# Halved first transposes, ScalarE key zeroing, one-step key copies and a new instruction order in a two-layer sliding-window attention and token-mixing kernel

## The chip, the cores and the metric

The kernel runs on one core of a Trainium2 chip. The metric is the device time of one execution in microseconds (us), the median of several runs. The core has five engines with a queue of instructions each: TensorE (PE in the profile, its weight loads PEld), VectorE (DVE), ScalarE (ACT), GpSimd (POOL) and SyncE (SP, which issues the DMAs here). Every queue is served in order; engines wait for each other through semaphores.

## The reference

```python
def _A_ref(x, wqkv, wo):                      # S=2048, D=512, H=32 heads of 16, window W=256
    q, k, v = split(x @ wqkv)
    scores = einsum("bhqd,bhkd->bhqk", q, k) * 16 ** -0.5
    scores = where(0 <= i - j < 256, scores, -1e9)
    return einsum("bhqk,bhkd->bhqd", softmax(scores), v) @ wo
def _B_ref(x, w1, b1, w2, b2):                # an MLP over the tokens, F=1792
    u = gelu(einsum("bsd,sf->bdf", layernorm(x), w1) + b1)
    return (einsum("bdf,fs->bds", u, w2) + b2).transpose(0, 2, 1)
for _ in range(2):
    x = x + _A_ref(layernorm(x), A_wqkv, A_wo)
    x = x + _B_ref(layernorm(x), B_w1, B_b1, B_w2, B_b2)
```

Inputs, weights and output are bfloat16; both layers use the same weights.

## The kernel before

The tokens are 16 blocks of 128 (`x_sb`, `xh_sb` after the layer norm). Four blocks make a group `m`. For each group `qkv` transposes the normalised blocks into `xhT`, multiplies them with the query, key and value weights (line 527, through `mm_group`), and copies the products out of PSUM. There are four head groups `o` of eight heads. Queries go to `qT` (lines 587 on VectorE, 589 on ScalarE). Keys go to `kbd`, where the two heads of each 32 rows stand in separate columns with zeros between: for the first group straight from PSUM, each head's columns multiplied with a 0/1 column `par` (line 598 on VectorE, two instructions, or 597 on ScalarE); for later groups by way of a staging tile `stg` (lines 609, 611) and then by POOL or VectorE (624) or by eight DMAs of SP (619). The DMAs write only what is not zero, so their tiles are zeroed once (`zero_keys`, line 506). Values go to `vst` (644, 646) and from there by DMA to `vb`.

Layer 0 takes its first group in two halves. Blocks 0 to 3 are transposed by TensorE through PSUM (line 563) and copied to `xhT` (572 on VectorE, 574 on ScalarE); all others are transposed by DMA (556). Before the first data come, TensorE multiplies a tile of ones (`f_warm`, line 397; `keep_warm`, line 404).

Attention goes over chunks of queries: 4, 4, 8, 8, 4 and 4 blocks of 64 in layer 0 and four times 8 in layer 1. For each chunk and head group TensorE makes scores (706), ScalarE the exponentials in passes of up to 1,024 columns (721, 152 in each layer), POOL multiplies the masked parts with 0/1 integers `ldm` (742), TensorE multiplies with the values (759), and VectorE and POOL transpose and divide (797, 801, 803, 808). The output product with `wo_sb` is added to `x_sb` (830), followed by the second layer norm (476, 479, 493, 500). The token MLP's first product is made in parts: `u_part` (527, summed up at 894, 896 and 898) runs between the scores of later chunks; `u_last` (909) takes the rest after the last attention chunk, followed by the GELU on ScalarE (924). `y_block` makes the second product and adds it to `x_sb` (950). Layer 0's output blocks `y` are made just ahead of layer 1's attention and between its scores.

The order of all this is not that of the program text. The text only lists operations with what they read and write, and for many of them which engines could take them (`alts`). `ORDER` is a packed list that gives, operation by operation, which comes next and on which engine; `replay` follows it, gives out tiles and PSUM banks from pools in that order, and `emit` writes one queue for each engine with the waits that the reads and writes need. The costs and priorities in the text have been used to make the list, and are not read when the kernel is built.

## Time and profile before

| | us |
|---|---|
| median of 3 runs | 434.19 |
| lowest, highest | 433.92, 434.27 |
| the profiled execution | 434.22 |
| its span in the trace | 432.5 |
| busy: PE, ACT, DVE, POOL | 413.7, 324.3, 302.8, 240.2 |

Times in the profile count from the start of the span. A row of the timeline gives start, length, engine, line, operation and tiles, how many instructions were merged, and in brackets how long the engine had been idle and what ended the idle time. In a group of instructions the number behind the bar is the busy time in us, and then the mean length of one in ns. In a table of stages, each engine's busy time is followed by its number of instructions.

### The profile page before, as it was taken

To read this page: it belongs to the slowest core of one execution; us is meant where nothing else is said; L and a number is where in the kernel's file an instruction comes from. 1 tells how busy PE (TensorE), PEld (TensorE's weight loads), DVE (VectorE), ACT (ScalarE), POOL (GpSimd) and SP (SyncE) were. 2 spreads that over 40 slices of the span, in tenths; PEclk is the share of its full clock that TensorE was granted. 3 is DMA by queue.
4 is the path that set the end of the run, shared out by engine and by line. 5 is a ranking of instruction groups with operands and counts; after the bars stand their busy time and mean duration, and the time that the engine had idled before them with its cause. 6 is when DMAs were issued, how large, how long until landed. Compare 5 with 4: busy or idle time off the path is not lost.

```text
span 432.5 us, 14247 instructions
## 1 busy us (share of the span) xinstructions
PE 413.7 (96%) x6120; PEld 188.5 (44%) x6192; DVE 302.8 (70%) x566; ACT 324.3 (75%) x375; POOL 240.2 (56%) x359
## 2 busy tenths in 40 slices
PE   8888999999999999999999999999999999999997
PEld 7444344443444444443444444443443444444454
DVE  7999988998789878647555877888876377421224
ACT  4999999999998965608989999999999960430000
POOL 5688969687797651012677589778784741000000
DMA  8744613540222446435353340320221455682353
GB/s 245 208 62 90 158 37 65 111 101 15 77 52 52 135 141 180 119 90 153 72 148 66 86 124 2 79 46 7 55 64 38 110 147 156 186 230 77 116 165 109
DMA packets 95023, 45.12 MB, mean 104 GB/s; under 512 B 27888, under 2 KB 94960, under 8 KB 94960
## 3 DMA queue, kind: packets, MB, share of 16 engines
q1 hardware_dynamic: 94960, 44.20, 39.9%
q8 instruction: 49, 0.80, 0.8%
q14 instruction: 14, 0.11, 0.1%
HBM read 33.56 MB, written 2.10 MB: 82 GB/s over the span
## 4 chain that ended last, share of the span: by engine, by line
PE 83%; ACT 8%; DVE 4%; issue 2%; POOL 1%; DMA 1%; SPq 0%
PE PS L527 58%; PE PS L706 10%; PE PS L759 8%; PE PS L909 8%; ACT pt L721 7%; POOL pt L742 1%; DVE xh_sb L500 1%; DMA x_sb<-in_A_x_dram 1%; DVE rl L797 1%; ACT kbd L597 0%; DVE x_sb L950 0%; DVE stats L476 0%; DVE uT L898 0%; DVE oT L808 0%; ACT vst L646 0%
## 5 line engine op out<-in xcount | busy, mean ns | idle before, releaser
L721 ACT ACTIVATE pt<-PS 128x1024 bf16<-128x1024 f32 (+1 forms) x304 | 282.8, 1031 | 9.5 <-PE PS L706 7.7
L742 POOL TENSOR_TENSOR pt<-pt,ldm 128x256 int32<-128x256 int32 (+2 forms) x266 | 176.5, 691 | 56.0 <-ACT pt L721 52.3
L527 PE MATMUL PS<-xh_sb,w1b 128*128 128x512 bf16 x273 | 68.9, 380 | 2.9 <-issue 2.3
L527 PE MATMUL PS<-uT,w2b 128*128 128x512 bf16 (+2 forms) x298 | 66.8, 359 | 1.0 <-issue 0.6
L527 PE MATMUL PS<-xhT,wqkv 128*128 128x512 bf16 (+1 forms) x272 | 64.2, 355 | 3.2 <-issue 1.7
L706 PE MATMUL PS<-qT,kbd 32*128 32x64 bf16 (+4 forms) x1552 | 60.2, 247 | 2.6 <-ACT pt L721 1.6
L950 DVE SCALAR_TENSOR_TENSOR x_sb<-PS,b2col,x_sb 128x512 bf16<-128x512 f32 x31 | 22.7, 747 | 55.7 <-PE PS L527 55.5
L493 POOL TENSOR_TENSOR rstd<-agg,mhalf 128x2 f32<-128x2 f32 (+1 forms) x34 | 23.5, 693 | 57.0 <-DVE agg L479 56.8
L706 PEld LDWEIGHTS PS<-qT,kbd 32*128 32x128 bf16 x1552 | 22.7, 92 | 61.2 <-ACT pt L721 44.8
L797 DVE STREAM_TRANSPOSE rl<-PS 128x1024 f32<-128x1024 f32 x31 | 38.5, 1242 | 14.1 <-PE PS L759 13.7
L759 PE MATMUL PS<-pt,vb 64*17 64x128 bf16 (+4 forms) x3104 | 44.0, 248 | 1.2 <-ACT pt L721 0.9
L476 DVE BATCH_NORM_STATS2 stats<-x_sb 128x6 f32<-128x512 bf16 x62 | 41.0, 676 | 1.4 <-DMA x_sb<-in_A_x_dram 1.1
L527 PEld LDWEIGHTS PS<-uT,w2b 128*128 128x128 bf16 x308 | 27.6, 98 | 31.9 <-issue 3.3
L527 PE MATMUL PS<-uT,pt 128*128 128x512 bf16 x164 | 40.1, 379 | 0.3 <-issue 0.2
L759 PEld LDWEIGHTS PS<-pt,vb 64*17 64x17 bf16 x3104 | 31.5, 84 | 17.9 <-ACT pt L721 6.2
L527 PEld LDWEIGHTS PS<-xh_sb,w1b 128*128 128x128 bf16 x292 | 24.6, 97 | 32.8 <-issue 5.4
L527 PEld LDWEIGHTS PS<-xhT,wqkv 128*128 128x128 bf16 x288 | 24.3, 97 | 28.8 <-issue 5.4
L909 PE MATMUL PS<-xh_sb,w1b 128*128 128x512 bf16 x154 | 34.7, 379 | 0.1
L527 PE MATMUL PS<-wqkv,xhT 128*128 128x512 bf16 x118 | 32.7, 381 | 1.9 <-ACT pt L721 1.1
L924 ACT ACTIVATE uT<-rl,b1col 128x512 bf16<-128x512 f32 x28 | 18.1, 711 | 21.7 <-DVE rl L920 21.5
L527 PE MATMUL PS<-wo_sb,oT 128*128 128x512 bf16 x118 | 31.5, 380 | 1.6 <-issue 0.8
L500 DVE TENSOR_SCALAR xh_sb<-x_sb,agg,rstd 128x512 bf16<-128x512 bf16 x64 | 28.7, 473 | 2.6 <-POOL rstd L493 2.5
(70 smaller groups left out, 330.5 us busy)
## 6 DMA issues: line engine op xcount, KB each, us to landing
w1b<-in_B_w_dram SPq DMA_DIRECT2D x109, 128.0 KB, 2.7
w2b<-in_B_w_dram SPq DMA_DIRECT2D x70, 128.0 KB, 2.8
pt<-in_B_w_dram SPq DMA_DIRECT2D x42, 128.0 KB, 3.0
vb<-vst SPq DMA_DIRECT2D x64, 68.0 KB, 2.1
out_dram<-x_sb SPq DMA_DIRECT2D x15, 128.0 KB, 1.9
x_sb<-in_A_x_dram SPq DMA_DIRECT2D x3, 512.0 KB, 7.5
wqkv<-in_A_wqkv_dram SPq DMA_DIRECT2D x4, 256.0 KB, 5.2
wqkv<-in_A_wqkv_dram SPq DMA_DIRECT2D x1, 512.0 KB, 6.6
```

Source lines behind the costliest of these rows:

```text
L476: op("vector:stat", lambda e: e.bn_stats(st[:, 0:6], bank(ft) if ft else x_sb[:, t, :]), reads=[ft or f"x{t}"], writes=[("st", i)], cost=d ...
L493: op("gpsimd:rstd", lambda e: e.tensor_tensor(rstd[:, t0:t1, 0], agg[:, t0:t1, 1], mhalf[:, 0:1].to_broadcast([P, t1 - t0]), op=ALU.pow), ...
L500: op("vector:xh", lambda e: e.tensor_scalar(xh_sb[:, t, :], x_sb[:, t, :], agg[:, t, 0:1], rstd[:, t, :], op0=ALU.subtract, op1=ALU.mult), ...
L527: return e.matmul(o, lhsT=w, rhs=x, start=start, stop=stop, skip_group_check=True)
L706: last = e.matmul(bank(tt[r // 2], r % 2)[:, base + c0 * 64:base + (c0 + n) * 64], lhsT=kbd[32 * r:32 * r + 32, tk[0][o].slot, jj].rearran ...
L721: op("scalar:exp", lambda e, ts=ts, tp=tp, i=i, cols=cols: e.activation(probs(tp)[:, i, 0:cols, :], pair(ts)[:, :, 0:cols].rearrange("p r ...
L742: return e.tensor_tensor(v, v, m, op=ALU.mult)
L759: last = e.matmul(bank(t, h)[32 * r:32 * r + 17, i + q0 * 64:i + (q0 + n) * 64], lhsT=vb[64 * h:64 * h + 64, tk[1].slot, jj, 4 * o + r, :] ...
L797: op("vector:od", lambda e, t=tod, tr=tr: e.transpose(rl[:, tr.slot:tr.slot + 2].rearrange("p a b -> p (a b)"), pair(t)), reads=[(tod, i) ...
L909: last = e.matmul(bank(tu, tt), lhsT=v()[:, sc - b0, k0 + tt * P:k0 + (tt + 1) * P], rhs=xh_sb[:, sc, :], start=(sc == b0), stop=(sc == NT ...
L924: op("scalar:gelu", lambda e, ft=ft, tt=tt: e.activation(uT[:, ft, :], rl[:, tmps[tt].slot], ACTF.Gelu_apprx_tanh, bias=b1col[:, ft:ft + 1 ...
L950: op("vector:resy", lambda e: e.scalar_tensor_tensor(x_sb[:, t, :], bank(ft), b2col[:, t:t + 1], x_sb[:, t, :], op0=ALU.add, op1=ALU.add), ...
```

## The change

- The transposes of blocks 0 and 1 and their copies to `xhT` are done in two halves of two 128-column pieces each, in banks of their own. The four copies are ScalarE's in the new list; before, one was ScalarE's and one VectorE's.
- The key and query products of the first half group for head group 0 are made 128 tokens at a time (16 matmuls of 128 columns for 8 of 256); the first 128 tokens' product reads block 0 alone.
- The zeroing of two thirds of `kbd` moves from POOL (two memsets after block 1's normalisation) to ScalarE (two copies of a zero, spread over 2,048 float32, right after the first table load).
- A first-group key copy on VectorE becomes one product of the PSUM tile, read twice, with `par`, instead of two instructions.
- The two sums that made `half` become four memsets of 64 rows, which need no other data. The last mask pieces and the ones of `vst` may go to the other of VectorE and POOL, and do. The warm-up has 36 matmuls instead of 40.
- `ORDER` is new, from the first instruction to the last. On SP the first key weights now go ahead of blocks 2 and 3, the value weights ahead of the second halves of the key and query weights. In all, ScalarE has 8 query copies less, 3 key stagings more and 3 value copies more (VectorE the reverse), and one copy of an MLP part less; POOL has 4 instructions of key spreading less, VectorE 6 more, and one key tile less is spread by DMA. Exponentials, masks and matmuls are the same in number, but for the halved first products and the warm-up.

```diff
--- before.py
+++ after.py
@@ -13,32 +13,33 @@
 
 
 ORDER = (
...
 )
 
 def begin_order(n):
@@ -393,7 +394,7 @@
         warm = Tile(banks)
 
         def f_warm(e):
-            for _ in range(40):
+            for _ in range(36):
                 last = e.matmul(PS[:, warm.slot, 0:P], lhsT=uT[:, 0, 0:P], rhs=uT[:, 0, 0:P], start=True, stop=True)
             return last
         def keep_warm(n, after):
@@ -443,13 +444,15 @@
 
 
         for h in range(2):
-            op("vector", lambda e, h=h: e.tensor_reduce(
+            f_par = lambda e, h=h: e.tensor_reduce(
                 par[:, h:h + 1], ident[:].rearrange("p (a b) -> p a b", b=32)[:, :, 16 * h:16 * h + 16],
-                axis=mybir.AxisListType.XY, op=ALU.add), reads=["ident"], writes=[("par", h)])
-            op("vector", lambda e, h=h: e.tensor_reduce(
-                half[:, h:h + 1], ident[:, 64 * h:64 * h + 64], axis=mybir.AxisListType.X, op=ALU.add),
-               reads=["ident"], writes=[("half", h)])
-        HALF = [("half", h) for h in range(2)]
+                axis=mybir.AxisListType.XY, op=ALU.add)
+            op("vector:par", f_par, reads=["ident"], writes=[("par", h)], cost=200)
+        for h in range(2):
+            for i in range(2):
+                f_half = lambda e, h=h, i=i: e.memset(half[64 * i:64 * i + 64, h:h + 1], float(i == h))
+                op("vector:half", f_half, writes=[("half", h, i)], cost=60)
+        HALF = [("half", h, i) for h in range(2) for i in range(2)]
         op("gpsimd", lambda e: e.memset(tri[:], 1.0), writes=["tri"], cost=200)
         op("gpsimd", lambda e: e.affine_select(tri[:], tri[:], pattern=[[-1, 192]], compare_op=ALU.is_ge, fill=0.0,
                                                base=31, channel_multiplier=1), reads=["tri"], writes=["tri"], cost=300)
@@ -459,8 +462,8 @@
                                                       op0=ALU.mult, op1=ALU.add), reads=["tri", "ld0"] + HALF,
            writes=["ld0"])
         for i, m, c in ((1, 1.0, 0.0), (2, -1.0, 1.0), (3, -1.0, 1.0)):
-            op("vector", lambda e, i=i, m=m, c=c: e.tensor_scalar(ldm[:, i, :], ldm[:, 0, :], m, c, op0=ALU.mult, op1=ALU.add),
-               reads=["ld0"], writes=[f"ld{i}"])
+            f_ld = lambda e, i=i, m=m, c=c: e.tensor_scalar(ldm[:, i, :], ldm[:, 0, :], m, c, op0=ALU.mult, op1=ALU.add)
+            op("vector:ldm", f_ld, reads=["ld0"], writes=[f"ld{i}"], cost=190, alts=[("gpsimd", f_ld, 280)])
         LD = [f"ld{i}" for i in range(4)]
 
         f_one = lambda e: e.memset(vst[:, :, :, :, 16:17], 1.0)
@@ -501,11 +504,6 @@
                                                       op0=ALU.subtract, op1=ALU.mult),
                reads=[f"x{t}", f"ag{t}", f"rs{t}"], writes=[f"xh{t}"], cost=dve_cost(512, 0.25, ptrs=2), lock=True)
 
-        def zero_keys():
-            for k in (1, 2):
-                op("gpsimd:zero", lambda e, k=k: e.memset(kbd[:, 4 * k:4 * k + 4].rearrange("p a b c d -> p (a b c d)").bitcast(dt.float32), 0.0),
-                   reads=["xh1"], writes=["kz0"], cost=1900)
-
         def filler(wide):
             return Tile(banks, 1, None if wide else "f")
 
@@ -554,24 +552,26 @@
                 t = 4 * m + i
                 if wide is None:
                     op("sync:tr", lambda e: e.dma_start_transpose(xhT[:, tx.slot, :, i * P:(i + 1) * P], xh_sb[:, t, :]),
-                       reads=[f"xh{t}"], writes=[(tx, i)], dma=True, cost=1700, issue=1600.0, prio=-1e5)
+                       reads=[f"xh{t}"], writes=[(tx, i, c) for c in range(4)], dma=True, cost=1700, issue=1600.0, prio=-1e5)
                     return
-                ft = filler(True)
-
-                def f_tr(e):
-                    for c in range(4):
-                        last = e.transpose(bank(ft).bitcast(dt.bfloat16)[:, c * P:(c + 1) * P],
-                                           xh_sb[:, t, c * P:(c + 1) * P], ident[:])
-                    return last
-                op("tensor:ftr", f_tr, reads=[f"xh{t}", "ident"], writes=[ft], cost=4 * 60, prio=fprio(),
-                   holds=[tx], cfg="f", cls="f")
-                if wide and not layer and m == 0:
-                    keep_warm((2, 8)[i], [g.ops[-1]])
-                src = lambda: bank(ft).bitcast(dt.bfloat16)[:, 0:512].rearrange("p (c n) -> p c n", c=4)
-                dst = lambda: xhT[:, tx.slot, :, i * P:(i + 1) * P]
-                op("vector:evt", lambda e: e.tensor_copy(dst(), src()), reads=[ft], writes=[(tx, i)],
-                   cost=dve_cost(512, 0.5, psum=True), prio=-2e5,
-                   alts=[("scalar", lambda e: e.copy(dst(), src()), act_cost(512))])
+                for c0, c1 in ((0, 2), (2, 4)) if wide and not layer else ((0, 4),):
+                    ft = filler(True)
+
+                    def f_tr(e, c0=c0, c1=c1, ft=ft):
+                        for c in range(c0, c1):
+                            last = e.transpose(bank(ft).bitcast(dt.bfloat16)[:, c * P:(c + 1) * P],
+                                               xh_sb[:, t, c * P:(c + 1) * P], ident[:])
+                        return last
+                    op("tensor:ftr", f_tr, reads=[f"xh{t}", "ident"], writes=[ft], cost=(c1 - c0) * 60, prio=fprio(),
+                       holds=[tx], cfg="f", cls="f")
+                    if wide and not layer and m == 0 and c1 == 4:
+                        keep_warm((2, 8)[i], [g.ops[-1]])
+                    src = lambda ft=ft, c0=c0, c1=c1: bank(ft).bitcast(dt.bfloat16)[:, c0 * P:c1 * P].rearrange("p (c n) -> p c n", n=P)
+                    dst = lambda c0=c0, c1=c1: xhT[:, tx.slot, c0:c1, i * P:(i + 1) * P]
+                    op("vector:evt", lambda e, src=src, dst=dst: e.tensor_copy(dst(), src()), reads=[ft],
+                       writes=[(tx, i, c) for c in range(c0, c1)],
+                       cost=dve_cost((c1 - c0) * P, 0.5, psum=True), prio=-2e5,
+                       alts=[("scalar", lambda e, src=src, dst=dst: e.copy(dst(), src()), act_cost((c1 - c0) * P))])
 
             def proj(o, which, a, b, wide):
 
@@ -579,10 +579,11 @@
                 ft = key[0]
                 at = lambda: bank(ft)[:, 0:n]
                 ts = Tile(p_stg) if which and m else None
-                mm_group("fk" if which else "fq", key, 4, lambda c: (
-                    at(), wqkv[:, c, which * 512 + o * P:which * 512 + (o + 1) * P], xhT[:, tx.slot, c, a:b]),
-                    [(tx, i) for i in range(a // P, b // P)] + [(f"w{which}", o)], cols=n, step=2 if n > 256 else 4,
-                    holds=([ts] if ts else []) + [tk[o]] if which else [tq[o]])
+                for a1, b1 in ((a, a + P), (a + P, b)) if wide and not layer else ((a, b),):
+                    mm_group("fk" if which else "fq", key, 4, lambda c, a1=a1, b1=b1: (
+                        bank(ft)[:, a1 - a:b1 - a], wqkv[:, c, which * 512 + o * P:which * 512 + (o + 1) * P], xhT[:, tx.slot, c, a1:b1]),
+                        [(tx, i, c) for i in range(a1 // P, b1 // P) for c in range(4)] + [(f"w{which}", o)], cols=b1 - a1, step=2 if b1 - a1 > 256 else 4,
+                        holds=([ts] if ts else []) + [tk[o]] if which else [tq[o]])
                 if which == 0:
                     op("vector:evq", lambda e: e.tensor_copy(qT[:, tq[o].slot, a:b], at()), reads=[key],
                        writes=[(tq[o], k) for k in KEYS(a, b)], cost=dve_cost(n, psum=True), prio=-2e5,
@@ -591,18 +592,22 @@
                 dst = lambda h: kbd[:, tk[o].slot, a // 64:b // 64, h, :]
                 if m == 0:
                     src = lambda: at().rearrange("p (s n) -> p s n", n=64)
-                    for hs in ([0], [1]) if wide and not layer else ([0, 1],):
-                        def f_ka(e, act=False, hs=hs):
-                            for h in hs:
-                                last = (e.activation(dst(h), src(), ACTF.Copy, scale=par[:, h:h + 1]) if act else
-                                        e.tensor_scalar(dst(h), src(), par[:, h:h + 1], 0.0, op0=ALU.mult, op1=ALU.add))
-                            return last
-                        two = [("vector", f_ka, len(hs) * dve_cost(n, psum=True, ptrs=1)),
-                               ("scalar", lambda e, f_ka=f_ka: f_ka(e, True), len(hs) * act_cost(n, 1))]
-                        if not wide or hs == [1]:
-                            two.reverse()
-                        op(two[0][0] + ":evka", two[0][1], reads=[key] + [("par", h) for h in hs],
-                           writes=[(tk[o], h, k) for h in hs for k in KEYS(a, b)], cost=two[0][2], prio=-3e5, alts=two[1:])
+                    heads = lambda x: x.rearrange("p s (h n) -> p s h n", h=1).to_broadcast([P, (b - a) // 64, 2, 64])
+
+                    def f_kv(e):
+                        return e.tensor_tensor(
+                            kbd[:, tk[o].slot, a // 64:b // 64], heads(src()),
+                            par[:].rearrange("p (s h n) -> p s h n", s=1, n=1).to_broadcast([P, (b - a) // 64, 2, 64]), op=ALU.mult)
+
+                    def f_ka(e):
+                        for h in range(2):
+                            last = e.activation(dst(h), src(), ACTF.Copy, scale=par[:, h:h + 1])
+                        return last
+                    two = [("vector", f_kv, dve_cost(2 * n, psum=True)), ("scalar", f_ka, 2 * act_cost(n, 1))]
+                    if not wide:
+                        two.reverse()
+                    op(two[0][0] + ":evka", two[0][1], reads=[key] + [("par", h) for h in range(2)],
+                       writes=[(tk[o], h, k) for h in range(2) for k in KEYS(a, b)], cost=two[0][2], prio=-3e5, alts=two[1:])
                     if wide:
                         first_k[0] = g.ops[-1]
                     return
@@ -638,7 +643,7 @@
                     sp, ft = sp0 + k, filler(m == 0)
                     mm_group("fv", ft, 4, lambda c, sp=sp, ft=ft: (
                         bank(ft), xhT[:, tx.slot, c, sp * P:(sp + 1) * P], wqkv[:, c, 1024:1536]),
-                        [(tx, sp)] + [("w2", o) for o in range(4)], holds=[tv, ts])
+                        [(tx, sp, c) for c in range(4)] + [("w2", o) for o in range(4)], holds=[tv, ts])
                     src = lambda ft=ft: bank(ft).rearrange("p (r h e) -> p h r e", h=2, e=16)
                     dst = lambda k=k: vst[:, ts.slots[k], :, :, 0:16]
                     op("vector:evv", lambda e, src=src, dst=dst: e.tensor_copy(dst(), src()), reads=[ft, "one"], writes=[(ts, k)],
@@ -658,8 +663,6 @@
                 late_stats[:] = [first_k[0]] if m == 0 and not layer and not first else []
                 before([4 * m + i for i in range(a // P, b // P)], first)
                 late_stats[:] = []
-                if first and not layer:
-                    zero_keys()
                 for i in range(a // P, b // P):
                     transpose(i, first if m == 0 and not layer else None)
                 for which in (1, 0):
@@ -955,6 +958,10 @@
         for layer in range(2):
             tqs, tks, tos, gate = {}, {}, {}, []
             op("scalar:tab", lambda e: e.preload_act_table_set("natural_log_exp_and_others"), writes=["acttab"], cost=1280)
+            for k in () if layer else (1, 2):
+                keys = lambda k=k: kbd[:, 4 * k:4 * k + 4].rearrange("p a b c d -> p (a b c d)").bitcast(dt.float32)
+                op("scalar:zero", lambda e, keys=keys: e.copy(keys(), stats[:, 0, 0, 6:7].to_broadcast([P, 2048])),
+                   reads=["eps0", "acttab"], writes=["kz0"], cost=1900, alts=[("gpsimd", lambda e, keys=keys: e.memset(keys(), 0.0), 1900)])
 
             def prepare(m):
                 def before(ts, wide):
```

53 lines of the change are left out of this document (27 added, 26 removed).

## The prediction

> **What bounds the kernel now.** I read the page first, then the busy time of each engine by stage, then ScalarE's instructions in order of time to find the edges of the stages, and last the start instruction by instruction.
>
> ```profile
> span 432.5 us, 14247 instructions
> PE 413.7 (96%) x6120; PEld 188.5 (44%) x6192; DVE 302.8 (70%) x566; ACT 324.3 (75%) x375; POOL 240.2 (56%) x359
> ACT  4999999999998965608989999999999960430000
> ...
> 12.00:20.00 8.00, 7.39 (x91) 3.97 (x89) 7.69 (x23) 7.98 (x12) 6.86 (x9) 1.00 0.75 212
> 20.00:40.00 20.00, 17.32 (x430) 8.45 (x430) 18.96 (x37) 19.57 (x23) 15.89 (x23) 1.00 0.43 72
> 60.00:80.00 20.00, 19.48 (x344) 8.32 (x347) 16.89 (x31) 19.45 (x22) 15.02 (x24) 1.00 0.38 69
> 120.00:140.00 20.00, 19.04 (x419) 8.04 (x403) 18.09 (x33) 18.38 (x21) 17.22 (x24) 1.00 0.21 50
> 140.00:160.00 20.00, 19.20 (x432) 9.22 (x437) 15.02 (x27) 18.25 (x20) 13.05 (x18) 1.00 0.43 120
> 260.00:280.00 20.00, 19.57 (x345) 8.42 (x347) 16.55 (x31) 19.59 (x23) 16.16 (x25) 1.00 0.18 40
> 380.00:400.00 20.00, 19.89 (x93) 9.00 (x94) 3.02 (x5) 2.73 (x5) 0.00 (x0) 1.00 0.53 150
> ```
>
> The columns of the stages are length, then busy time of PE, PEld, DVE, ACT, POOL. "ACT 75%" hides two kinds of stage. In both attentions ScalarE is busy 19.45 to 19.59 of 20 us, and VectorE is nearly as full in the first of them (18.96). In the MLP stages ScalarE does next to nothing and TensorE runs 19.89 of 20. TensorE's 96% is no proof that it binds everywhere: a busy matmul may be waiting in its pipe. So I treat an attention as a queue of ScalarE work and an MLP as a queue of matmuls; the edges are the first and last exponentials of each layer:
>
> ```profile
> 9.68 1.02 ACT L721 ACTIVATE pt<-PS 128x1024 bf16<-128x1024 f32 x1
> 157.63 1.94 ACT L721 ACTIVATE pt<-PS 128x1024 bf16<-128x1024 f32 x2 [0.22 <-PE PS L706]
> 198.37 1.94 ACT L721 ACTIVATE pt<-PS 128x1024 bf16<-128x1024 f32 x2
> 344.51 5.61 ACT L721 ACTIVATE pt<-PS 128x1024 bf16<-128x1024 f32 x6
> ```
>
> That cuts the span into a start (to 9.68), attention 0 (to 157.63 + 1.94 = 159.57), MLP 0 up to layer 1's first exponential (198.37), attention 1 (to 344.51 + 5.61 = 350.12) and the tail (to 432.5). The profiled execution took 434.22, 1.7 more than its span; the median of the three runs is 434.19, so a change of the span is read as a change of the time.
>
> **The start.** Ten rows carry it:
>
> ```profile
> 0.78 1.28 ACT L957 ACT_TABLE_LOAD   x1 [0.78 <-PEq L1017]
> 4.99 0.21 DVE L456 TENSOR_SCALAR ldm<-tri,half 128x64 int32<-128x64 bf16 x1
> 5.12 0.41 DVE L500 TENSOR_SCALAR xh_sb<-x_sb,agg,rstd 128x512 bf16<-128x512 bf16 x1
> 6.02 0.59 ACT L574 COPY xhT<-PS 128x512 bf16<-128x512 bf16 x1 [3.95 <-PE PS L563]
> 6.69 0.41 DVE L572 COPY xhT<-PS 128x512 bf16<-128x512 bf16 x1
> 7.80 1.21 PEld L527 LDWEIGHTS PS<-xhT,wqkv 128*128 128x128 bf16 x12 [0.33 <-DMA wqkv<-in_A_wqkv_dram]
> 7.80 0.84 ACT L597 ACTIVATE kbd<-PS,par 128x256 bf16<-128x256 f32 x2 [1.19 <-PE PS L527]
> 8.53 0.37 ACT L589 CAST qT<-PS 128x256 bf16<-128x256 f32 x1
> 9.22 0.40 PE L706 MATMUL PS<-qT,kbd 32*128 32x256 bf16 x12
> 12.48 1.29 DVE L476 BATCH_NORM_STATS2 stats<-x_sb 128x6 f32<-128x512 bf16 x2 [0.21 <-DMA x_sb<-in_A_x_dram]
> ```
>
> The second block's copy ends at 6.69 + 0.41 = 7.10, the keys follow, and then TensorE waits until 7.80 for the query weights to land. This wait is what the halves run into. In the new program the query weights are still fifth in SP's queue, behind the same bytes (blocks 0 and 1, the first key weights, blocks 2 and 3; the last two have changed places), so I leave their landing at 7.80.
>
> Step by step in the new lists: the mask instruction at 4.99 goes ahead of the statistics, so block 0 is normalised some 0.1 earlier. All four half copies are ScalarE's. Its casts of 256 columns take 0.37, and the next instruction after such a cast starts 0.27 later (row at 10.64 below). Begun at about 5.9, with the second pair when block 1's transposes come at 6.5, they end near 7.2: where VectorE ended at 7.10. The halves therefore give nothing here, and cost at most 0.1. The first key product ends at about 7.7 and its copies run 7.8 to 8.6, as now. The query product begins at 7.80 again, eight matmuls of 128 columns for four of 256, and the same streamed columns. What changes is behind it: only one key group, not two, stands before the first score, and VectorE, not ScalarE, copies the queries (8.5 to 8.9). ScalarE no longer has the second key pair either. I get scores at 9.05 for 9.22 and the first exponential at 9.5: **−0.2**.
>
> In SP's queue the second half of the query weights falls from seventh to ninth, behind the value weights and blocks 4 to 7. The same bytes ended at 12.48 for those blocks, so it lands there; its first score feeds ScalarE's fourth group, at 15.5 or later (two full passes, two half ones, two value copies, two full passes after 9.5): hidden. The output weights fall behind four transposes; the first product with them waits for the first chunk's outputs.
>
> Zeroing on ScalarE: two copies of 2,048 float32. The nearest rows are the POOL memset of the same tile and ScalarE's pass over 1,024 elements twice:
>
> ```profile
> 6.23 1.80 POOL L506 MEMSET kbd<- 128x2048 f32 x1 [0.51 <-DVE xh_sb L500]
> 13.02 1.80 POOL L506 MEMSET kbd<- 128x2048 f32 x1
> 10.64 0.37 ACT L589 CAST qT<-PS 128x256 bf16<-128x256 f32 x1
> 9.43 1.65 DVE L598 TENSOR_SCALAR kbd<-PS,par 128x256 bf16<-128x256 f32 x4
> L898 DVE TENSOR_TENSOR uT<-PS,uT 128x512 f32<-128x512 f32 x14 | 9.4, 672 | 4.0 <-PE PS L527 4.0
> L624 POOL TENSOR_SCALAR kbd<-stg,par 128x512 bf16<-128x512 bf16 x30 | 20.4, 695 | 1.4 <-DVE stg L609 1.2 <-ACT stg L611 0.2
> ```
>
> One copy is thus 1.80 to 1.94, both 3.6 to 3.9, from the table load's end at 2.06 to 5.7 or 6.0. Behind them on ScalarE stands the first half copy, at about 5.9; behind that TensorE. I take 1.85 each, an end at 5.8, and nothing lost; the worst is 0.1. Without the 3.95 idle before ScalarE's first copy it would cost all 3.7.
>
> One-step key copies: two VectorE instructions of 0.41 (1.65 for four) become one product of 512 written elements, nearest to the addition from PSUM of 512 at 0.672: 0.15 less per tile, seven tiles in layer 0, about 1 us of VectorE. The new order spends it: over both layers eight query copies leave ScalarE for VectorE, and three stagings and three value copies come back. Constants (the two sums replaced by four small memsets, the mask signs moved to POOL) lie before the first block's data or under the first exponentials: nothing.
>
> **Attention 0.** Between the first and the last exponential the old list gives ScalarE one narrow query copy, four wide ones and three value copies; the new one four key stagings, one wide query copy and three value copies.
>
> ```profile
> 107.49 0.61 ACT L589 CAST qT<-PS 128x512 bf16<-128x512 f32 x1
> 120.15 0.59 ACT L646 CAST vst<-PS 128x512 bf16<-128x512 f32 x1
> 294.64 0.62 ACT L611 CAST stg<-PS 128x512 bf16<-128x512 f32 x1
> 195.87 1.27 ACT L597 ACTIVATE kbd<-PS,par 128x512 bf16<-128x512 f32 x2 [4.16 <-PE PS L527]
> 385.54 10.74 PE PS L527 x49
> ```
>
> Eight against eight, a narrow one (0.27) replaced by a wide one (0.6): **+0.3**, as ScalarE is full.
>
> **MLP 0.** A group of two matmuls is 2 x 10.74 / 49 = 0.44. From the last score to the key group that releases the copy at 195.87 the old list has 47 output and 2 value groups, the new one 46 and 4; the rest is equal: one group more, 0.44. ScalarE now has two value copies right before the key copy, which are done about 0.1 late: **+0.5**.
>
> **Attention 1.** ScalarE's other instructions inside it are 13 before (2 value copies, a key activation, 5 query, 2 staging, 3 MLP) and 12 after (4, 1, 3, 1, 3): one less, **−0.6**. **The tail** keeps eight MLP groups behind the last score, not ten: 2 x 0.44, **−0.9**, as long as TensorE has work until the last four blocks are normalised. If that chain decides, it is 0.
>
> Sum: −0.2 + 0.3 + 0.5 − 0.6 − 0.9 = −0.9, 434.2 − 0.9 = **433.3**. Upwards the tail's term may be 0 and copies and zeroing cost 0.1 each; downwards the first score may be ready with its keys (8.6) instead of its queries (8.9), 0.3 earlier: 433.0 to 434.4.
>
> **The rivals.** *VectorE becomes the bound of the first chunks (slower).* It is 18.96 of 20 full between 20 and 40 us. Up to the 32nd exponential the new list has four query copies more and one statistic more on it, and is 1.1 us longer by the rows above (one-step copies included). If every us of lateness becomes a wait of a score, that is +1.1 there and again about 1 while later key and query copies stay late: 433.3 + 2.1 = 435.4. For it speaks the fullness; against it that by the 64th exponential the new list is 1.7 shorter again. It decides once ScalarE falls below 19 of 20 in that stage.
>
> *POOL's relief shortens the waits (faster).*
>
> ```profile
> L759 PEld LDWEIGHTS PS<-pt,vb 64*17 64x17 bf16 x3104 | 31.5, 84 | 17.9 <-ACT pt L721 6.2 <-POOL pt L742 6.1 <-issue 3.9
> 0.86 0.08 DVE L470 MEMSET stats<- 128x24 f32 x1 [0.86 <-PEq L1017]
> 0.91 0.17 DVE L407 MEMSET uT<- 128x128 bf16 x1
> 1.10:2.10 1.00, 0.96 (x10) 1.00 0.27 40
> 4.60:5.10 0.50, 0.50 (x10) 1.00 1.03 309
> ```
>
> The value products wait 6.1 us for POOL's masks. POOL loses 3.6 of zeroing and four instructions of key spreading (2.8). From 120 to 160 ScalarE idles 1.62 + 1.75; if a third of that goes, and ScalarE's list keeps its place in attention 1, some 1.1 more comes off: 432.2. Against it: early masks are not what the first scores wait for.
>
> *The array is slow at the first products.* The last two rows (length, PE busy, clock, DMA) show warm-up matmuls at about 0.1 us apiece at the start and 0.05 later, with a granted clock of 1.00 in both. The new warm-up waits for five more VectorE memsets, four of 0.08 and one of the size that took 0.17, so starts some 0.5 later, and has four matmuls less. If the fast rate comes after the first products, the queries' eight matmuls cost 0.4 more and the key group about 0.4: scores 0.5 to 0.8 later, 433.9 (0.6). [...]
>
> *The change does not do what it says:* the query weights still end the wait and the rest is equal work in other places: 434.2.
>
> **How the numbers follow.** Measurement tells about 0.2% (0.87 us) from no change: faster is below 433.3, slower above 435.1. The forecast has 0.40, half on each side of the lower bound; POOL's relief 0.22; the full VectorE 0.25, all slower; the slow array 0.08 and the empty change 0.05, both same. Faster 0.42, same 0.33, slower 0.25. The range goes from 431.2 (POOL's relief at twice its price) to 435.9 (VectorE's a quarter dearer).
>
> **What would show it.** The query weights' wait near 7.8 and the first exponential at 9.4 to 9.6 show the start right; before 9.2 means that the weights landed earlier, after 9.8 a slow array or late zeroing. ScalarE at 19.5 in each 20 us of both attentions shows the queue reading right, and below 19 between 20 and 40, with VectorE releasing the scores, the slower rival. First exponential of layer 1 at 198.6, the last at 349.7, and 81.5 behind it, would show the three later terms. I am wrong if one stage moves by over 2 us.

## The result and the profile after

The changed kernel takes **434.38 us** (median; 433.93 to 435.46) where the kernel before, run beside it, takes 433.81 (433.44 to 434.27): a ratio of 1.0017, 95% interval 1.0010 to 1.0024. It is slower by 0.57 us; the forecast was 0.9 faster. The profiled executions stand at 435.03 (span 433.3) and 434.22 (432.5), so the new one lies 0.65 above its own median and the old one 0.4.

The page of the new kernel: busy times, the chain of work that ended last, and the costliest group.

```profile
PE 423.1 (98%) x6196; PEld 188.1 (43%) x6196; DVE 305.8 (71%) x568; ACT 326.6 (75%) x375; POOL 232.8 (54%) x354
PE 75%; ACT 19%; DVE 3%; DMA 2%; SPq 1%; issue 0%
L724 ACT ACTIVATE pt<-PS 128x1024 bf16<-128x1024 f32 (+1 forms) x304 | 282.2, 1030 | 12.8 <-PE PS L709 10.7
```

The exponentials (line 724 now) have 12.8 us of idle time ahead of them, 10.7 of it released by scores. TensorE's rise to 98% is no finding: the trace of before has 6,120 matmul records, this one 6,196. The record of e7 below, whose order of work is the old one and whose records are complete, has 422 us too. It stands in for the kernel before wherever TensorE is counted. Busy time is here the time of overlapping records: those of 512 columns are 0.38 us long and begin 0.216 us apart.

The exponentials cut each execution into five stages (us):

| | first exponential | attention 0 | MLP 0, to layer 1's first | attention 1 | behind the last | span |
|---|---|---|---|---|---|---|
| before | 9.68 | 149.89 | 38.80 | 151.75 | 82.38 | 432.5 |
| after | 9.15 | 152.21 | 39.28 | 151.09 | 81.54 | 433.3 |
| difference | -0.53 | **+2.32** | +0.48 | -0.66 | -0.84 | +0.8 |
| forecast | -0.2 | +0.3 | +0.5 | -0.6 | -0.9 | -0.9 |

In this execution four of five terms came out near the forecast, and one stage ate all of them. Of its 2.32 us, 0.53 is only the earlier first exponential; the last one ends 1.79 later (161.36 for 159.57). The 112th still begins level with the kernel before (117.35 for 117.25), so nearly all of the loss is made behind it. The busy times of the engines there, after the change (columns as in the prediction; before, ScalarE had 18.38 and 18.25):

```profile
120.00:140.00 20.00, 18.34 (x458) 8.00 (x462) 18.21 (x32) 17.54 (x19) 13.79 (x20) 1.00 0.26 70
140.00:160.00 20.00, 19.73 (x440) 8.69 (x439) 15.75 (x27) 17.61 (x19) 12.74 (x18) 1.00 0.32 87
```

The timeline of ScalarE in these last chunks of attention 0 after the change (start, length, instructions, count; in brackets the wait ahead and what ended it):

```profile
134.96 1.94 ACT L724 ACTIVATE pt<-PS 128x1024 bf16<-128x1024 f32 x2 [0.51 <-PE PS L709]
137.75 1.94 ACT L724 ACTIVATE pt<-PS 128x1024 bf16<-128x1024 f32 x2 [0.85 <-PE PS L709]
140.36 1.94 ACT L724 ACTIVATE pt<-PS 128x1024 bf16<-128x1024 f32 x2 [0.67 <-PE PS L709]
...
154.65 1.94 ACT L724 ACTIVATE pt<-PS 128x1024 bf16<-128x1024 f32 x2 [0.84 <-PE PS L709]
157.25 1.94 ACT L724 ACTIVATE pt<-PS 128x1024 bf16<-128x1024 f32 x2 [0.66 <-PE PS L709]
```

Over the whole of attention 0 ScalarE's instructions other than exponentials are eight in both kernels, as the prediction counted them (4.68 us before, 5.14 after); its idle time went from 5.2 to 7.6. TensorE and VectorE at the first of these waits, after the change:

```profile
135.05 0.60 PE L525 MATMUL PS<-xh_sb,w1b 128*128 128x512 bf16 x2
136.05 1.04 PE L525 MATMUL PS<-xh_sb,w1b 128*128 128x512 bf16 x4 [0.40 <-DVE xh_sb L503]
137.30 0.40 PE L709 MATMUL PS<-qT,kbd 32*128 32x192 bf16 x12 [0.21 <-DVE rl L800]
...
151.93 2.33 PE L525 MATMUL PS<-xh_sb,w1b 128*128 128x512 bf16 x10
154.19 0.41 PE L709 MATMUL PS<-qT,kbd 32*128 32x64 bf16 x24
```

```profile
131.91 0.18 DVE L482 BATCH_NORM_AGGREGATE agg<-stats 128x2 f32<-128x9 f32 x1
132.02 0.65 DVE L479 BATCH_NORM_STATS2 stats<-x_sb 128x6 f32<-128x512 bf16 x1
132.70 0.20 DVE L482 BATCH_NORM_AGGREGATE agg<-stats 128x2 f32<-128x9 f32 x1
...
134.29 1.70 DVE L503 TENSOR_SCALAR xh_sb<-x_sb,agg,rstd 128x512 bf16<-128x512 bf16 x2
```

The same place in e7, VectorE and then TensorE:

```profile
130.84 0.68 DVE L478 BATCH_NORM_STATS2 stats<-x_sb 128x6 f32<-128x512 bf16 x1
...
134.03 0.41 DVE L502 TENSOR_SCALAR xh_sb<-x_sb,agg,rstd 128x512 bf16<-128x512 bf16 x1
```

```profile
150.92 1.89 PE L524 MATMUL PS<-xh_sb,w1b 128*128 128x512 bf16 x8
```

Scores stand in TensorE's list behind MLP groups, and these wait for the normalisation of the later blocks (line 503), whose last statistic begins at 132.02; in e7 it begins at 130.84. The last of these normalisations is also longer, 1.08 us for 0.41, with a mask product of POOL beside it:

```profile
134.91 1.08 DVE L503 TENSOR_SCALAR xh_sb<-x_sb,agg,rstd 128x512 bf16<-128x512 bf16 x1
```

```profile
134.80 1.04 POOL L745 TENSOR_TENSOR pt<-pt,ldm 128x384 int32<-128x384 int32 x1
```

Later ten MLP matmuls stand ahead of one score; in e7, there are at most eight.

The start, with the waits that the prediction named:

```profile
2.15 3.83 ACT L963 COPY kbd<-stats 128x2048 f32<-128x2048 f32 x2
5.89 1.20 ACT L574 COPY xhT<-PS 128x256 bf16<-128x256 bf16 x4
7.58 0.84 ACT L604 ACTIVATE kbd<-PS,par 128x256 bf16<-128x256 f32 x2 [0.49 <-PE PS L525]
9.15 1.94 ACT L724 ACTIVATE pt<-PS 128x1024 bf16<-128x1024 f32 x2 [0.73 <-PE PS L709]
```

### The profile page after: what moved, and what is told of

Same layout as the page of the kernel before. It is cut to its first block, busy times and chain, and to the rows that moved or that the text cites. A ratio compares the mean times of both kernels' runs of the same rounds, so it can differ in the third digit from the quotient of the medians.

```text
span 433.3 us, 14319 instructions
## 1 busy us (share of the span) xinstructions
PE 423.1 (98%) x6196; PEld 188.1 (43%) x6196; DVE 305.8 (71%) x568; ACT 326.6 (75%) x375; POOL 232.8 (54%) x354
## 4 chain that ended last, share of the span: by engine, by line
PE 75%; ACT 19%; DVE 3%; DMA 2%; SPq 1%; issue 0%
PE PS L525 53%; ACT pt L724 19%; PE PS L709 8%; PE PS L912 8%; PE PS L762 7%; DMA wqkv<-in_A_wqkv_dram 2%; DVE rl L800 1%; DVE kbd L629 0%; DVE xh_sb L503 0%; SPq L423 0%; SPq L419 0%; DVE w2b L897 0%; ACT vst L651 0%; DVE x_sb L953 0%; DVE w2b L901 0%
## 5 line engine op out<-in xcount | busy, mean ns | idle before, releaser
L724 ACT ACTIVATE pt<-PS 128x1024 bf16<-128x1024 f32 (+1 forms) x304 | 282.2, 1030 | 12.8 <-PE PS L709 10.7
L525 PE MATMUL PS<-xh_sb,w1b 128*128 128x512 bf16 x292 | 73.7, 381 | 0.9 <-DVE xh_sb L503 0.4
L525 PE MATMUL PS<-uT,w2b 128*128 128x512 bf16 (+2 forms) x308 | 70.5, 360 | 0.1
L525 PE MATMUL PS<-xhT,wqkv 128*128 128x512 bf16 (+2 forms) x296 | 68.5, 352 | 1.4 <-ACT pt L724 0.9
L525 PE MATMUL PS<-uT,pt 128*128 128x512 bf16 x168 | 41.9, 379 | 0.0
L912 PE MATMUL PS<-xh_sb,w1b 128*128 128x512 bf16 x156 | 34.3, 379 | 0.0
L525 PE MATMUL PS<-wo_sb,oT 128*128 128x512 bf16 x128 | 33.5, 381 | 0.3 <-ACT pt L724 0.3
```

The costliest lines, as they stand in the source:

```text
L525: return e.matmul(o, lhsT=w, rhs=x, start=start, stop=stop, skip_group_check=True)
L724: op("scalar:exp", lambda e, ts=ts, tp=tp, i=i, cols=cols: e.activation(probs(tp)[:, i, 0:cols, :], pair(ts)[:, :, 0:cols].rearrange("p r ...
L912: last = e.matmul(bank(tu, tt), lhsT=v()[:, sc - b0, k0 + tt * P:k0 + (tt + 1) * P], rhs=xh_sb[:, sc, :], start=(sc == b0), stop=(sc == NT ...
```

## The experiments

Unless a diff says otherwise, each kernel has the new text, and only its list ORDER is edited. Theory 1: the new order loses the time in the last chunks of attention 0. Theory 2: the new text (halves, zeroing, split products) costs it. Theory 3: TensorE is busy all the time, so only the sum of its matmuls counts. Theories 4 to 6 came up on the way; the expectation of a run states them.

### e1 to e4: text and order taken apart

```diff
 e1:  ORDER = old order throughout
 e2:  ORDER = new order to exponential 32, then old
 e3:  ORDER = old order into MLP 0, then new
 e4:  ORDER = new to exponential 32, old into MLP 0, then new
```

> The new program text under the order of the kernel before, operation by operation, each on the engine that it had before (key zeroing back on POOL, second block's half copies on VectorE, half pieces one after the other). What stays of the change is the text alone: halved transposes, copies and first products, one-step key copies on VectorE, memsets for the sums, 36 warm-up matmuls. Theory 1 (the loss is the new order's, in the last two chunks of layer 0's attention, where MLP matmuls stand ahead of scores that ScalarE waits for): within 0.3 us of before, 433.5 to 434.0, and attention 0 (first to last exponential) at 149.9 as before. Theory 2 (a part of the text itself costs the 2.3 us in attention 0, the halved or one-step forms above all): some 435, attention 0 near 152.

> The new kernel's order up to the 32nd exponential, where it is 1.3 us ahead, and the order of before from there. Theory 1: the lead is kept as long as ScalarE stays full; some of it goes where the two orders spread ScalarE's copies differently, so 432.6 to 433.3. Rival, theory 3 (attention 0 is held by the matmuls that must fit into it, so that what is gained early comes back as waits of ScalarE later): the last exponential of layer 0 ends at 159.6 as before, and the time is 433.8.

> The order of before up to the first matmuls of layer 0's MLP behind its attention, and the new order from there. Theory 1: start and attention 0 as before (9.7, 149.9), MLP 0 0.5 longer, attention 1 0.7 and the tail 0.8 shorter: 433.8 - 1.0 = 432.8. Theory 3 says the same of these stages, unless the gain of the tail was a loan from attention 0; then 433.8.

> Both splices: the new order up to the 32nd exponential, the order of before up to layer 0's MLP, the new order from there. If the stages add up (theory 1): 433.8 - 0.6 to 1.2 - 1.0 = 431.6 to 432.2. Theory 3: 432.8, the start's gain being lost.

Medians 435.63, 435.09, 436.79 and 435.48 (before: 433.81): all slower than expected. Two reasons are no theory's. First, at the joint in MLP 0 of e3 and e4, where sums and gelus fall out of step, that stage took 41.1 and 40.8. Second, the start of e1 and e3 (10.26, and 11.87 in e3) shows something new, below. Neither holds for e2 (9.20, MLP 0 38.80). The profiled executions of e1, e2 and e4 were each the fastest of their runs, 0.7 to 0.9 below the median, so what makes these medians is not shown. What does follow: attention 0 took 150.05 and 150.09 in e1 and e3, against 152.21, so the text costs nothing there (theory 2 falls for that stage), the order does. And attention 1 and the tail of e3 and e4 come near the new values (151.37 and 151.10; 81.54 and 81.55).

The timeline of e1, VectorE, then POOL, then TensorE:

```profile
5.21 1.86 DVE L502 TENSOR_SCALAR xh_sb<-x_sb,agg,rstd 128x512 bf16<-128x512 bf16 x1 [0.23 <-POOL rstd L495]
```

```profile
5.12 1.80 POOL L963 MEMSET kbd<- 128x2048 f32 x1
```

```profile
7.13 0.40 PE L561 MATMUL PS<-ident,xh_sb 128*128 128x128 bf16 x4 [1.58 <-DVE xh_sb L502]
```

The normalisation of block 1, 0.41 us otherwise, took 1.86, as long as POOL's memset beside it. The old text let the memset wait for that very normalisation (it read xh1); the new text dropped the wait, and old order with new text puts the two side by side.

### e7 and e8: the zeroing alone

```diff
 e7, from e1:   order: the two zeroings behind ScalarE's table load
-               engine of the two zeroings: POOL
+               engine of the two zeroings: ScalarE
 e8, from the new kernel:
-               engine of the two zeroings: ScalarE, behind the table load
+               engine of the two zeroings: POOL, behind the second reciprocal root
```

> As e1 (new text in the old order), with one thing changed: the two zeroings of the key tiles are ScalarE's, right behind the table load, instead of POOL's. Theory 4 (in e1 the POOL memset, which no longer waits for block 1's normalisation, ran beside it and stretched it from 0.41 to 1.86 us, which left TensorE idle for 1.6 us and cost the start): block 1's normalisation takes 0.41, TensorE has no gap over 0.5 us before the first key products, the first exponential comes at 9.5 to 9.8 instead of 10.26, attention 0 stays 150.1: span 432.4, median about 434.0 and less spread than e1's 1.9. Theory 2 (the half copies and the 128 column products themselves cost the start): still 10.2, 435.6.

> The mirror of e7: the new kernel in its own order, but with the two zeroings back on POOL, behind the second block's reciprocal root, where nothing makes them wait for block 1's normalisation. Theory 4: block 1's normalisation takes 1.8 instead of 0.41, the first exponential comes at 10.2 to 10.6 for 9.15, and the span is 0.5 to 1.2 longer than 433.3. Theory 2: the start stays within 0.2 of 9.15.

e7: median **433.95** (433.63 to 434.24), ratio 0.9999 (0.9991 to 1.0008); normalisation 0.41, first exponential 9.45, attention 0 150.01. e8: first exponential 10.26 for 9.15, span 433.9, one run of 435.69. VectorE in e8:

```profile
5.44 1.86 DVE L503 TENSOR_SCALAR xh_sb<-x_sb,agg,rstd 128x512 bf16<-128x512 bf16 x1 [0.33 <-POOL rstd L496]
```

Theory 4 stands both ways: the normalisation takes 1.86 us beside the memset (e1, e8) and 0.41 without it (e7, and the new kernel). How the memset lengthens it, no run shows. And e7 settles theory 2: the whole new text in the old order is worth 0.0. The change is its order.

### e5, e6, e9, e10: the old order put back in parts

```diff
 e5:  ORDER = new to exponential 128, old to the end of MLP 0, new
 e6:  ORDER = new to exponential 32, old to the end of MLP 0, new
 e9:  ORDER = new to exponential 112, old to the start of MLP 0, new
 e10: ORDER = old to the start of MLP 0 (zeroing as e7), new
```

> The new kernel's order up to the 128th exponential and in layer 1 and the tail; between them, from the 128th exponential of layer 0 to the end of MLP 0, the old order. Theory 1 (the loss is made where the new order puts MLP groups ahead of the late scores, and nothing pays for it later): attention 0 ends 1.6 us earlier, at 159.7 for 161.4, MLP 0 takes 38.8, attention 1 151.1, the tail 81.6: span 431.2, about 1.6 below the new kernel's median, 432.8. Theory 3 (TensorE is busy 97 to 98% of the span, so a matmul that leaves one stage only stands in another): attention 0 ends 1.6 earlier but MLP 0, attention 1 and the tail together take 1 to 1.6 longer: 434.0 to 434.4.

> As e4, but the old order now holds until the key products of layer 1, so that no gelu of MLP 0 is reordered at the joint. Theory 1: the first exponential at 9.1, attention 0 150.6, MLP 0 38.8 (not 40.8), attention 1 151.1, tail 81.6: span 431.2, time 432.9, faster than both kernels by about 1. Theory 3: what MLP 0 gains is given back in attention 1 and the tail: span 432.5 to 433, time 434.3.

> As e5, but the old order comes in at the 112th exponential instead of the 128th, so that VectorE's statistics of the later blocks are the old ones too, and the new order returns at the beginning of MLP 0 instead of its end. Theory 5 (the new order makes VectorE finish the normalisation of the later blocks about 1.2 us late between 128 and 136 us, and TensorE, which has no slack there, loses 1.3 to 1.7 us waiting for it and for the scores behind; MLP 0 and the tail lose and gain nothing, matmuls only change stages): TensorE's lag between 130 and 170 us grows by 9.5 as in e7, not by 11.8 as in the new kernel; span 431.6 to 432.2, median 433.2 to 433.8. Theory 3 in its strict form (only the sum of the matmuls counts, whatever waits where): 434.4, as the new kernel.

> The start and attention 0 of e7 (old order, zeroing on ScalarE), the new order from the beginning of MLP 0 to the end. Theory 5: start and attention 0 as e7 (9.45, 150.0), MLP 0 39.3, attention 1 151.1, tail 81.6; of these only attention 1's 0.6 is a wait less, the others are matmuls in other places: span 431.5, median 433.2 to 433.4, below both kernels. Theory 3, strict: 433.9, as e7.

Medians 434.73, 434.01, 434.98 and 433.85. e5 and e9 missed: at each change of order ScalarE waited 1.07 us (e5, 137.6) and 1.62 (e9, 120.3), as I read it because the old list counts on work that the new one has not done by then, and the gain behind it only paid for that. They decide nothing. e6 and e10 come out beside the old kernel, not 0.5 to 1 us below. In e6 MLP 0 rose to 39.66 with 249 matmuls in it for 245 in e7, and TensorE idle for 0.02 us: matmuls that only changed stage, as theory 3 says. In e10 attention 1 gave its gain (151.23 for 151.73), but its profiled start was at 9.96 for 9.45; whether that start is behind its median too is not shown.

### e11, e12: which engine paces attention

```diff
 e11, in mm_group:
-                    for k in range(k0, k1):
+                    for k in range(k0, k1):     # one of two left out in 16 "fu" steps
 e12:
-                        op("scalar:exp", ... cols=cols ...
+                        op("scalar:exp", ... cols=cols // 2 for the 57th to 64th ...
```

> The new kernel with 16 of the MLP matmuls left out that stand between the scores of attention 0 (the 512 column products of blocks 8 to 11; the output lacks them), 16 x 0.2165 = 3.46 us of TensorE. If TensorE sets the pace of attention: attention 0 and the span 2.9 to 3.5 us shorter, median 431.0 to 431.5. If ScalarE sets it, as the prediction had it (busy 19.5 of 20): ScalarE idles about 1 us in that stretch (exponentials 64 to 96), so the span falls by at most 1: 433.4 to 434.4.

> The new kernel with 8 of the exponentials of attention 0 (57th to 64th) cut to half their columns (the other half is left as it was), 8 x about 0.43 = 3.4 us of ScalarE less. If ScalarE sets the pace of attention: the span 2.5 to 3.4 shorter, 431.0 to 431.9. If TensorE sets it: less than 0.5 shorter, 433.9 to 434.4, and ScalarE idles 3 us more.

435.06 (434.12 to 436.52) and 434.99 (433.59 to 435.68): neither a gain. The edit of e11 did not fall where its expectation puts it. A count of the MLP matmuls between the exponentials of both traces has the 16 missing ones between the 124th and the 144th, from 130 to 149 us, and none in the stretch from the 64th to the 96th; that the exponentials from the 64th to the 128th keep the new kernel's times to 0.01 us (all 0.25 later) says nothing. It tells something else, for it thins out the very chunks that lose the time. TensorE there, with one and two matmuls in the places of two and four:

```profile
135.30 0.39 PE L525 MATMUL PS<-xh_sb,w1b 128*128 128x512 bf16 x1
136.31 0.60 PE L525 MATMUL PS<-xh_sb,w1b 128*128 128x512 bf16 x2 [0.61 <-DVE xh_sb L503]
137.55 0.40 PE L715 MATMUL PS<-qT,kbd 32*128 32x192 bf16 x12 [0.64 <-DVE rl L806]
```

TensorE idles longer ahead of the score, which waits for VectorE's transposition behind the late normalisation, and ScalarE waits 0.86 us for it, as in the new kernel (0.85). So this wait is VectorE's lateness and not the number of MLP matmuls. Of the 3.46 us left out, 0.4 is gained by the 152nd exponential and 2.4 is more idle time of TensorE in attention 0 (7.5 us for 5.1); MLP 0 then took 39.99 for 39.28. In e12 (the halved exponentials are the 55th and the 57th to 63rd in the trace) ScalarE is busy 3.1 us less in attention 0 and idles 2.2 more, and from the 36th exponential to the 152nd only 0.07 us is gained. ScalarE's timeline windows (length, busy, count, clock, DMA share, GB/s), the new kernel's first, then e12's:

```profile
60.00:80.00 20.00, 19.75 (x23) 1.00 0.51 79
```

```profile
60.00:80.00 20.00, 16.81 (x22) 1.00 0.51 76
```

So a ScalarE that is busy 19.75 of 20 us does not set the pace there by itself: with 2.9 us less to do, it waits. TensorE is busy 19.56 and 19.55 of 20 us in that stretch; whether taking work from TensorE there would gain anything, no run shows.

### e13, e14, e15: the last chunks without a joint

The instructions that the new kernel issues between two of its exponentials stay the same set; inside, they stand in the old kernel's relative order.

```diff
 e13: ORDER[exp 120 .. exp 152] = sorted(same instructions, by place in the old order)
 e14: ORDER[exp 120 .. exp 136] = the same
 e15: ORDER[exp 136 .. exp 152] = the same
```

> The new kernel; only the instructions that it issues between its 120th and its 152nd exponential, the same set, stand there in the relative order of the old kernel, so nothing is done earlier or later at either end. Theory 5 (late normalisation and MLP groups ahead of scores cost attention 0 1.5 to 2.1 us in this window): the window is 1.2 to 2.0 us shorter, so is the span: 431.3 to 432.1, median 432.6 to 433.3. Theory 6 (the order of the window costs nothing by itself: in the new order some of the window's work is left over, and whatever order it has, the window takes as long): within 0.4 of the new kernel, 434.0 to 434.8.

> The same with the first half of the window only (120th to 136th exponential: the residual sums, statistics and normalisation of blocks 8 to 11 and the first MLP groups on them). Theory 5: the normalisation is done about 1 us earlier, TensorE's waits of 0.35, 0.40 and 0.21 there go, 0.6 to 1.2 us: median 433.2 to 433.8. Theory 6: 434.0 to 434.8.

> The same with the second half only (136th to 152nd exponential: MLP groups between scores, up to ten matmuls in a row in the new order, at most eight in the old). Theory 5: ScalarE's waits of 0.84 and 0.66 fall to 0.3 each, 0.6 to 0.9 us: median 433.5 to 433.8. Theory 6: 434.0 to 434.8.

e13: median **433.62** (433.05 to 434.02), 0.76 below the new kernel; ratio to the kernel before 0.9990 (0.9982 to 0.9999). Its exponentials keep the new kernel's times to 0.15 us up to the 124th and run 1.22 us ahead at the 148th; that lead is 1.16 at layer 1's first and 0.99 at the last. ScalarE there:

```profile
135.38 3.77 ACT L724 ACTIVATE pt<-PS 128x1024 bf16<-128x1024 f32 x4 [0.36 <-PE PS L709]
139.75 1.94 ACT L724 ACTIVATE pt<-PS 128x1024 bf16<-128x1024 f32 x2 [0.59 <-PE PS L709]
...
153.87 1.94 ACT L724 ACTIVATE pt<-PS 128x1024 bf16<-128x1024 f32 x2 [0.24 <-PE PS L709]
156.03 1.94 ACT L724 ACTIVATE pt<-PS 128x1024 bf16<-128x1024 f32 x2 [0.23 <-PE PS L709]
```

The halves missed: e14 436.30 (436.04 to 436.92), e15 435.64 (434.33 to 435.98). Each removes the waits that it aimed at and makes larger ones in the other order's part: e14's exponentials keep step with e13's to the 132nd (0.55 earlier throughout), then come waits of 0.51, 0.52 and 1.27 us (the last at 147.30). So theory 5 holds for the window, but not as a sum of separate waits: its two halves are worth less than nothing apart, and what each wait costs by itself is not shown. Theory 3 in its strict form falls with e13: the same matmuls, 0.76 us less.

### e16: the first weights earlier

```diff
-  SP: x0 x1 x2 wk wq
+  SP: x0 x1 wk wq x2
```

> e10 (old layer 0, new layer 1), with the key and query weights' loads ahead of the third load of x in SP's queue, since TensorE waits for them at 7.5. If the weights' landing sets the first exponential: 0.3 to 0.5 earlier, about 9.3, and as later starts were carried unchanged to the end, the median falls by as much, to 433.3 to 433.6, and its spread below 1 us. If not (blocks 4 to 7 come later and take it back before the 36th exponential): 433.8.

Median 434.26 (433.58 to 437.19): a miss. VectorE, TensorE, and the windows of TensorE in the profiled execution (length, busy, count, granted clock):

```profile
7.64 0.69 DVE L479 BATCH_NORM_STATS2 stats<-x_sb 128x6 f32<-128x512 bf16 x1 [1.81 <-DMA x_sb<-in_A_x_dram]
8.26 0.47 DVE L571 COPY xhT<-PS 128x256 bf16<-128x256 bf16 x2
```

```profile
8.78 3.11 PE L525 MATMUL PS<-xhT,wqkv 128*128 128x128 bf16 x20 [1.83 <-DVE xhT L571]
```

```profile
7.00:8.00 1.00, 0.00 (x0) 1.00 1.03 272
```

In this execution a statistic that waits for the delayed block stands in VectorE's list ahead of a half copy of block 1, and TensorE waits for the copy. It took 436.35 us, 2.1 above the median; whether the others waited as long is not shown.

## Why the prediction was wrong

**The step that failed is the term of attention 0.** It counted ScalarE's instructions (eight against eight, +0.3, measured +0.46) and closed with "as ScalarE is full". The count was right and the conclusion wrong: ScalarE was full only as long as each score came in time, and 1.62 + 1.75 us of idle time between 120 and 160 stood quoted in the prediction's own rival. I never compared the two lists of TensorE and VectorE in that stretch. e13 prices the order there: 1.2 us in the profile, of the 1.79 by which attention 0 ends late, and 0.76 in the median, more than the whole loss of 0.57 against the kernel before. Which waits in the stretch make it is shown in part: the one ahead of 137.75 is VectorE's (e11), the two behind 150 stand behind the run of ten matmuls and fall to 0.28 and 0.24 in e15.

A ledger shows where it goes: the TensorE work that e7 has begun by then and this kernel has not, each matmul counted at the median spacing of its shape in e7 (0.216 us for 512 columns, so that steps of 0.2 are one matmul). It rises where TensorE waits longer than in e7 (us):

| at | 20 | 100 | 180 | 300 | 360 | 420 |
|---|---|---|---|---|---|---|
| after | +0.1 | -0.4 | **+1.7** | +1.3 | +1.1 | +1.1 |
| e13 | +0.2 | -0.4 | +0.7 | +0.7 | +0.2 | +0.1 |

**The start** (-0.2) came as said and more: ScalarE's zeroing ends at 5.98, the first half copy starts at 5.89 (forecast about 5.9; ends and starts overlap in these rows), the four end near 7.1 (7.2), one-step key copies take 0.68 (0.672). The weights landed at 7.55 for 7.80, and "before 9.2 means that the weights landed earlier" held; but e7, in the old order, has them at 7.56 too, so this is not the change's doing. The size is one execution's: the eleven profiled kernels with this start (the new one, e2, e4 to e6, e9, e11 to e15) have their first exponential between 9.00 and 9.76, six of them by 9.36. And it is no gain: the matmuls before the first exponential are 88 for 92 in e7 and stand in attention 0 (2,868 for 2,864), and the ledger at 20 us is no lower. With the old order behind the new start (e2, e4, e6) attention 0 ends at 159.62 to 159.94, no earlier than in the kernel before or e7 (159.57, 159.46). Moving a matmul over the border of a stage moves the border, not the end.

**MLP 0** (+0.5, measured +0.48) and **the tail** (-0.9, measured -0.84) were sized right, and for the same reason are worth nothing: 247 matmuls for 245 and 482 for 485 in e7, with the ledger level to one matmul in both. The prediction's sum took relocated work for saved work. **Attention 1** (-0.6, measured -0.66) is the one term that is time in the ledger, which falls by about half a us in both rows from 180 to 360 us, with one instruction less on ScalarE (13 others for 14; the prediction counted the two of a key activation as one). No median shows it: e10, with the old layer 0 and this attention 1, stands at 433.85 beside e7's 433.95.

**The rivals.** The full VectorE (435.4) had the right sign and the right engine in a part of it, but the wrong place: between 20 and 40 us ScalarE is busy 19.44 of 20, above its point of decision; the loss is in the last chunks, where 120 to 140 and 140 to 160 have 17.54 and 17.61 for 18.38 and 18.25. POOL's relief did not show: those are the stretches that it was to fill. The slow array did not strike the profiled execution of the new kernel: in its warm-up, from 1.87 to 5.74, matmuls of 128 columns begin 0.107 us apart up to 5.36 and 0.056 from 5.46 (before: up to 4.84 and from 4.93; granted clock 1.00 in both kernels), and the first key product begins at 6.64. Nor did the 0.73 later warm-up cost anything there; e3 and e16 below show that slow first products have a price (first exponentials at 11.87 and 12.49). The rule given for being wrong, one stage moved by over 2 us, is what happened, though 0.53 of the 2.32 is the moved border.

Open: the runs of the new kernel spread over 1.5 us, those of e7 over 0.6. A later start is kept to the end in part (e8 starts 1.11 later than the new kernel, 0.55 of it is left from the 36th exponential on), so differences in the start would do: in the eleven profiled kernels with the new start the 24th exponential comes between 29.45 and 30.26. No run ties the spread to one transfer.

## What to carry to other kernels

A count of one engine's instructions prices a new order only if the other engines' lists feed it in time: compare, stretch by stretch, what stands ahead of each score, not only how much there is. Where two engines are both full, cut the execution by work done and not by events of one of them; work that crosses such a border looks like a gain on one side and a loss on the other. And test a stretch of an order by permuting the same set of instructions inside it: splices made waits as large as the effect. Then check in the trace that an edit fell where it was meant to: e11's did not.

## What had not been expected of the hardware

A memset of 1.80 us on POOL stretched a VectorE normalisation of 0.41 us that ran beside it to 1.86 (e1, e3, e8), as if it had waited for it. The 1.08 of the normalisation beside POOL's mask product of 1.04, shown with the result, looks like the same; in e7 and e13 nothing runs on POOL at that place, and it takes 0.41 and 0.40. No run moved that product alone.

In two profiled executions TensorE's granted clock halved behind short gaps ahead of the first products; its mean over the whole execution is 0.996 in these two and 1.00 in all others. In e3, with gaps of 0.47 and 1.58 us before 7.2, and in e16, with one of 1.83 before 8.8, it fell to 0.50 for about 3.4 us; these rows are e16's, 0.12 + 3.00 + 0.30 us at half the clock (length, busy, count, granted clock, DMA share, GB/s):

```profile
8.00:9.00 1.00, 0.22 (x3) 0.94 0.97 330
9.00:10.00 1.00, 1.00 (x13) 0.50 1.08 362
10.00:11.00 1.00, 1.00 (x7) 0.50 1.01 343
11.00:12.00 1.00, 1.00 (x9) 0.50 1.09 373
12.00:13.00 1.00, 1.00 (x18) 0.85 1.11 366
```

The first exponential came at 11.87 and 12.49. The same gap of 1.58 in the profiled execution of e1 left it at 1.00, with 10.26. What sets the slow spell off is open.
